# Mean and scale of a LayerNorm spread through DRAM instead of by TensorE's transposes

## The chip, the cores and the metric

The kernel runs on one core of one Trainium2 chip. The metric is device microseconds of one execution; the time of a kernel is the median of its runs. Before the change it is 1457.64 us, the median of three runs (1456.2 to 1458.19).

The core's engines work side by side, each on its own instructions in order: PE (TensorE, matrix products into PSUM), DVE (VectorE, elementwise), ACT (ScalarE, functions and copies), POOL (GpSimd, elementwise, SBUF only) and SP (SyncE, which here issues nearly all DMAs). An instruction that needs another engine's result waits at the head of its engine's queue, and everything behind it waits too.

## The reference

One sequence of 2048 rows of 576 features, all float32:

```python
xn = layernorm(x)                       # over the 576 features, eps 1e-5
q, k, v = split(xn @ wqkv)              # 32 heads of 18 features
pq, pk = phi(q), phi(k)                 # t + 1 where t > 0, else exp(t); + 1e-6
kv = einsum("bhsd,bhse->bhde", pk, v);  z = sum over s of pk
o = (pq @ kv) / (pq . z + 1e-6)         # linear attention, not causal
s = o @ wo
g = silu((gelu(xn @ w_gate) * (xn @ w_up)) @ w_down)
out = x + s * g
```

## The kernel before

The 2048 rows are 16 tiles of 128 rows; four tiles are a block (`TB` = 4 blocks of `TBN` = 512 rows). Products that must be exact to float32 are made from two words: an operand is cut into a high word in a fast matmul type (made by ACT) and a rest (made by DVE with a subtraction), and seven products of words make one of float32 (`PASSES`, `KV_PASSES`). Some short products are plain float32 instead.

**Stage 1** (lines 1328 to 1520) normalises the tiles and makes keys, values and the sum `kv`. For tiles 8 to 15, which the change touches, it does the following per tile t, in `kv_tile` (line 492):

- `x_mm(t, 0)`, `x_mm(t, 1)`, `x_mm(t, 2)`: 14 matmuls each on PE, xn of the tile times a third of the key and value weights, each into a PSUM bank of its own.
- `k_post(t, 0)` and `k_post(t, 1)`: DVE reads the keys out of the banks twice (once for the exponential, `e_k`, once for the positive part, `pk`); after the second, ACT makes the exponential of the whole tile and POOL adds it to `pk`.
- `v_post(t, 1)` and `v_post(t, 2)`: ACT copies the values from the banks to `va`, and some query columns to `qt`; POOL sets a column of ones in `va`.
- `turn(t + 1)`: see below; `place(t + 1)`, which for these tiles is `normalize` (line 228): DVE subtracts the mean from the tile (128 x 768), multiplies each half by the scale (128 x 384, twice), ACT casts the high words of the halves (`hi`), and DVE makes the four rests. `x_mm(t + 1, 0)` needs this.
- In an even tile, after `x_mm(t, 0)`, `kv_pair(t)`: for the two tiles before, `kv_mm` multiplies `pk` by `va` into the accumulator `kv_a`: five groups of heads, each in two halves, the fifth group with a short operand (36 columns, not 72). These are plain float32 products. They need POOL's `pk` and ACT's `va` of both tiles.

From tile 4 on, x comes twice: as rows (for the statistics) and transposed by the host (for the products), in one buffer for two tiles. `load_x(n, 2)` fetches tiles n and n + 1; two buffers alternate, so tiles 12 and 13 are fetched behind tile 8, into the buffer of tiles 8 and 9. Statistics run over the rows: `spread(n0, 2)` has DVE take mean and variance of two tiles (`bn_stats`, `bn_aggr`) and ACT a first inverse root; `scales(n0)` improves it with three small DVE instructions. Then mean and scale of a tile are columns, one number per partition; but in the transposed x a row of the tile runs along the free axis, so the two columns must become rows, equal in all partitions. `turn` does that: two 128 x 128 transposes on PE of a column broadcast to a square, into one PSUM bank `ms`, which `normalize` reads.

Statistics of tiles 12 and 13 are taken by `x_next(12)` at the end of tile 10, those of 14 and 15 by `x_next(14)` at the end of tile 12 (line 1509).

Between tiles 7 and 8 lie the query products of blocks 0 and 1 (`q_store`, line 540: PE makes them, DVE, ACT and POOL apply phi into a `gl` buffer, SP stores it to DRAM). Work of other engines is hung behind single products by the table `behind` (line 1492): there are the statistics of tiles 8 and 9 and of 10 and 11, the turn and place of tile 8, and the forms `T1` to `T4`, sums of x that are cut into words and stored. `form("T4")` runs at the end of tile 9 (line 1511): an ACT cast of 128 x 1536 and two DVE rests. Behind tile 15 follow the query products of blocks 2 and 3 with the table `ahead` (line 1521), the attention output, and then the long gate, up and down products, which take the rest of the span.

The order on every engine is the order of the program text: each helper (`act`, `vec`, `mm`, `pool`, `dma`, lines 122 to 135) pins its instruction in program order. Buffers come from pools by tag: `bank` has six PSUM banks, `gl` six SBUF buffers of 2 KB per partition, `slot` four (in this stage `pk` and `va` of two tiles). A first write to a reused buffer waits for the last reader of its former tile.

Of the kernel before, what the change touches and what calls it, by code (L numbers as in the profile page):

```python
# [8 lines left out]
F32 = mybir.dt.float32  # L9
# [7 lines left out]
P = 128  # L17
# [9 lines left out]
TT = TBN // P  # L27
# [64 lines left out]
def block_kernel(ctx, tc, x, xe, xt, wq_d, wkv_d, wo, wgu_d, wd_d, out):  # L92
# [76 lines left out]
    def spread(n0, n):  # L169

        bn = sb.tile([P, TT, 12], F32, tag="bn", bufs=2, name=f"bn_{n0}")
        mv = sb.tile([P, 2 * TT, 2], F32, tag="mv", bufs=4, name=f"mv_{n0}")
        for t in range(n):
            xs = xstat[(n0 + t) // 2][:, (n0 + t) % 2]
            for j in range(2):
                src = xs[:, j, 0:HALF] if n0 < TT else xs[:, j * HALF : (j + 1) * HALF]
                vec("bn_stats", out=bn[:, t, 6 * j : 6 * j + 6], in_=src)
            vec("bn_aggr", out=mv[:, t, :], in_=bn[:, t, :])
        st = sb.tile([P, 6, TT], F32, tag="st", bufs=4, name=f"st_{n0}")
        act(st[:, 0, 0:n], mv[:, 0:n, 1], AF.Ln, bias=eps_t)  # L180
        act(st[:, 2, 0:n], st[:, 0, 0:n], AF.Exp, scale=-0.5)
        vec("tensor_scalar", st[:, 1, 0:n], mv[:, 0:n, 1], LN_EPS, None, op0=ALU.add)
        mom[n0] = n, mv, st

    def scales(n0):

        n, mv, st = mom.pop(n0)
        v, r, c = (st[:, i, 0:n] for i in range(1, 4))
        if n == 1:
            vec("tensor_scalar", c, r, r, -0.5, op0=ALU.mult, op1=ALU.mult)  # L190
            vec("tensor_scalar", c, c, v, 1.5, op0=ALU.mult, op1=ALU.add)
            vec("tensor_scalar", c, c, r, None, op0=ALU.mult)
        else:
            vec("scalar_tensor_tensor", c, r, -0.5, r, op0=ALU.mult, op1=ALU.mult)
            vec("tensor_mul", c, c, v)
            vec("scalar_tensor_tensor", c, c, 1.5, r, op0=ALU.add, op1=ALU.mult)
        for t in range(n):
            scale_of[n0 + t] = mv[:, t, 0:1], c[:, t : t + 1]

    def center(n):  # L200

# [6 lines left out]
    def turn(n, new=bank):  # L208

        xs = xstat[n // 2][:, n % 2]  # L210
        if n >= TT:
            xts[n] = t = bank(f"ms_{n}")
            for i, v in enumerate(scale_of.pop(n)):
                pin(nc.tensor.transpose(  # L214
                    t[:, i * P : (i + 1) * P], v.to_broadcast([P, P]), ident
                ))
            return
        tiles = [new(f"xt_{n}_{j}") for j in range(2)]
        xts[n] = [t[:, 0 : 3 * P].rearrange("p (k t) -> p k t", k=3) for t in tiles]
        for j in range(2):  # L220
            for k in range(3):
                pin(nc.tensor.transpose(xts[n][j][:, k, :], xs[:, j, k * P : (k + 1) * P], ident))
# [4 lines left out]

    def normalize(n, s, b, c):

        ms = xts.pop(n)  # L230
        xs = xstat[n // 2][:, n % 2, D:].rearrange("p (k t) -> p k t", k=6)
        m, r = (ms[:, None, i * P : (i + 1) * P] for i in range(2))
        vec("tensor_sub", xs, xs, m.to_broadcast([P, 6, P]))
        for j, nm in enumerate(BS[b]):
            if nm not in xo[s]:
                xo[s][nm] = big(2 * b + j, [P, 5, TBN], F32R, f"xo_{s}_{nm}")
                new_plain(s, nm)
            vec(
                "tensor_mul", xf[s][nm][:, :, c], xs[:, 3 * j : 3 * j + 3],
                r.to_broadcast([P, 3, P]),  # L240
            )
        for nm in BS[b]:
            to_operand(xo[s][nm], xf[s][nm], c)
# [32 lines left out]
        if last:  # L276
            xts.pop(n)

    mom, scale_of, xts = {}, {}, {}

    def to_operand(o, src, c):
        act(o[:, 0:3, c], src[:, :, c], AF.Copy)
# [110 lines left out]
        act(e, e, AF.Exp, scale=-1.0)  # L393
        pool("tensor_add", o, o, e)

    def kv_mm(t):
        if t == 0:
            acc.append(own_bank("kv_a"))
        pk, va = pks.pop(t), vas.pop(t)
        for gi, wdt in enumerate(WIDTHS):  # L400
            for half in range(2):
                o, cs = kv_out(gi, half)
                mm(
                    o, va[:, 2 * gi + half, 0 : o.shape[0]],
                    pk[:, gi * GW + cs.start : gi * GW + cs.stop],
                    start=(t == 0 and gi == 0), stop=(t == S // P - 1),
                    skip_group_check=True,
                )
# [8 lines left out]
    def x_mm(t, c, js=(0, 1), passes=KV_PASSES):  # L417

        tb, i = divmod(t, TT)
        s, b = divmod(tb, 2)  # L420
        begin = (t, c) not in pkv
        if begin:
            pkv[t, c] = bank(f"kv_{t}_{c}")
        o = pkv[t, c]
        for j in js:
            for n, (wi, xi) in enumerate(passes):
                mm(
                    o[:, 0 : TW[c]], xo[s][BS[b][j]][:, xi, i * P : (i + 1) * P], kv_part(c, j, wi),
                    start=(begin and j == 0 and n == 0), stop=(j == 1 and (wi, xi) == (2, 2)),
                )  # L430
# [61 lines left out]
    def kv_tile(t, mid_=(), end=()):  # L492

        ahead = t % (2 * TT) != 2 * TT - 1
        x_mm(t, 0)
        if t % 2 == 0:
            kv_pair(t)
        if ahead:
            turn(t + 1)
        k_post(t, 0)  # L500
        x_mm(t, 1)
        if ahead:
            place(t + 1)
            save(t + 1)
        run(list(mid_))
        k_post(t, 1)
        v_post(t, 1)
        x_mm(t, 2)
        run(list(end))
        v_post(t, 2)  # L510

    def kv_pair(t):

        for i in (t - 2, t - 1):
            if i in vas:
                kv_mm(i)

    ph, ph_d = {}, {}

# [958 lines left out]
    def form_apart(nm):  # L1478
# [11 lines left out]
        dma(out=d[:, 2], in_=last[:, 0].bitcast(F32))  # L1490

    behind = {
        (0, 0): [lambda: kv_pair(N0), lambda: spread(N0, 2), lambda: difference(0, 3)],
        (0, 1): [
            lambda: scales(N0), lambda: form("T1"), lambda: q_store(1, 4),
        ],
        (0, 2): [lambda: form_apart("T3")],
        (0, 3): [lambda: turn(N0)],
        (1, 0): [lambda: place(N0)],
# [5 lines left out]
            run(behind.get((tb, gi), []))  # L1505
    for n in range(N0, 2 * N0):
        ends = []
        if n < 2 * N0 - 2:
            ends.append(lambda n=n: center(n + 2) if n == N0 else x_next(n + 2))
        if n == N0 + 1:  # L1510
            ends.append(lambda: form("T4"))
        if n == 2 * N0 - 3:
            ends.append(load_wo)
        if n == 2 * N0 - 2:
            ends.append(make_sel)
        if n == 2 * N0 - 1:
            ends += [lambda i=i: difference(1, i) for i in range(3)]
        kv_tile(n, end=ends)
        if n in (N0, N0 + 2):
            load_x(n + 4, 2)  # L1520
    ahead = {
        (2, 0): [lambda: kv_pair(2 * N0), kv_done, spread_sel, lambda: difference(1, 3)],
        (2, 1): [lambda: kv_wo(4), lambda: q_hold(2, 7, 4)],
        (2, 2): [lambda: kv_wo(0), lambda: kv_wo(1), move_rows],
        (2, 3): [lambda: kv_wo(2), lambda: kv_wo(3)],
        (3, 0): [lambda: den(2), lambda: q_hold(3, 8, 4)],
# [117 lines left out]
```

## Time and profile before

| | |
|---|---|
| median of three runs | 1457.64 us |
| profiled execution, its own time | 1456.24 us |
| span of the profiled execution | 1454.5 us |
| PE busy | 1447.7 us, 100% of the span |
| DVE, ACT, POOL busy | 79%, 39%, 40% |
| DMA moved | 233.98 MB, 161 GB/s over the span |
| granted TensorE clock | 1.00 |

The profile is one execution. Its page gives the busy time of each engine and the groups of instructions that cost most; the trace behind it can be asked for a timeline. A row of a timeline has the start (us from the span's start), the time, the engine, the line of the program, the operation, `out<-in` by the program's names, the shapes, and how many instructions are merged in the row; in brackets stands how long the engine sat idle before it and what ended that. A line is that of the helper (L126 is `vec`, L123 `act`, L132 `pool`, L129 `mm`, L214 the transposes of `turn`), so rows are told apart by their names. Plain float32 products leave two records each: a pair of 20 products shows as x40. A matmul's time runs until its result has left the array, so rows overlap; the distance between starts is what a matmul costs. In the page, "chain that ended last" follows back what released each step.

In time: the query products of blocks 0 and 1 end at 106.6 us, tile 8 begins there, tile 15 ends at 175.2 us.

### The profile page before, as it was taken

How to read it: one execution, taken by the hardware profiler on the slowest of the kernel's cores; microseconds unless marked ns; L12 is line 12 of the kernel's file. 1: busy time of each engine (PE TensorE's matmuls, PEld its weight loads, DVE VectorE, ACT ScalarE, POOL GpSimd, SP SyncE). 2: the span in 40 equal slices, each digit the busy share in tenths (PEclk: the TensorE clock that was granted, in tenths of full speed). 3: DMA queues.
4: the chain of work that ended last, by engine and by line, in shares of the span. 5: the costliest groups of instructions: out<-in, count | busy, mean ns of one | idle time of the engine just before them, and what ended most of it. 6: DMA issues, size and time to landing. Idle time of an engine off the chain costs nothing.

```text
span 1454.5 us, 22180 instructions
## 1 busy us (share of the span) xinstructions
PE 1447.7 (100%) x8286; PEld 1289.9 (89%) x8286; DVE 1149.5 (79%) x1605; ACT 561.3 (39%) x914; POOL 579.6 (40%) x520
## 2 busy tenths in 40 slices
PE   9999999999999999999999999999999999999998
PEld 8989989988888888888888888888889999999998
DVE  7787767376787887888777878778888978989888
ACT  6343355332222233322332232332235555545454
POOL 3342340235756567566475755667632000000000
PEclk9999999999999999999999999999999999999999
DMA  5543105521422315224242243323389887767886
GB/s 223 191 190 141 38 30 212 209 109 51 169 98 104 130 51 182 94 94 140 72 159 87 98 149 106 113 85 118 129 277 349 262 263 251 249 188 232 278 289 224
DMA packets 118085, 233.98 MB, mean 161 GB/s; under 512 B 11018, under 2 KB 44682, under 8 KB 116058
## 3 DMA queue, kind: packets, MB, share of 16 engines
q1 hardware_dynamic: 115178, 220.31, 45.0%
q0 software_dynamic: 2656, 12.06, 2.2%
q8 instruction: 65, 1.06, 0.3%
q14 instruction: 42, 0.34, 0.1%
q10 hardware_dynamic: 144, 0.20, 0.0%
HBM read 149.91 MB, written 82.58 MB: 160 GB/s over the span
## 4 chain that ended last, share of the span: by engine, by line
PE 98%; DVE 1%; ACT 0%; issue 0%; POOL 0%; DVEq 0%; ACTq 0%; POOLq 0%
PE bd L129 25%; PE al L859 16%; PE de L859 16%; PE ga L859 16%; PE kv L129 8%; PE be L859 8%; PE s L129 4%; PE q L129 4%; PE kv_a L129 1%; PE idle L129 0%; PE d L129 0%; PE kw L129 0%; PE b L129 0%; PE ms L214 0%; DVE acc L126 0%
## 5 line engine op out<-in xcount | busy, mean ns | idle before, releaser
L132 POOL TENSOR_TENSOR sm<-raw 128x384 f32<-128x384 f32 x72 | 75.2, 1044 | 145.9 <-DMA raw<-in_wgu_dram 120.6
L129 PE MATMUL kv<-wkv,xo_B 128*128 128x412 f32 (+2 forms) x662 | 125.7, 348 | 0.0
L129 PEld LDWEIGHTS kv<-wkv,xo_B 128*128 128x128 f32 x662 | 119.8, 188 | 1.4 <-DVE wkv L126 0.5
L126 DVE TENSOR_TENSOR wa<-sm,wa 128x768 fp32r<-128x768 f32 x72 | 92.3, 1282 | 36.1 <-ACT wa L123 35.2
L129 PE MATMUL bd<-w_head,hi 128*128 128x288 f32 x516 | 117.9, 294 | 0.0
L126 DVE TENSOR_TENSOR wb<-raw,wb 128x256 fp32r<-128x256 f32 (+1 forms) x108 | 102.1, 946 | 7.4 <-ACT wb L123 5.8
L126 DVE TENSOR_TENSOR wa<-raw,wa 128x256 fp32r<-128x256 f32 x72 | 66.3, 921 | 51.7 <-ACT wa L123 50.6
L123 ACT ACTIVATE hi<-raw_h 128x1024 fp32r<-128x1024 f32 x59 | 62.5, 1060 | 94.8 <-PE bd L129 64.8
L129 PE MATMUL bd<-w_end,hi 128*128 128x288 f32 x448 | 89.8, 294 | 0.0
L123 ACT ACTIVATE spot_h<-spot_h 128x512 f32<-128x512 f32 x49 | 30.7, 633 | 150.3 <-DVE spot_h L126 150.3
L129 PEld LDWEIGHTS bd<-w_head,hi 128*128 128x128 f32 x516 | 87.0, 188 | 0.1
L126 DVE TENSOR_TENSOR raw_h<-raw_h,hi 128x1024 fp32r<-128x1024 f32 x59 | 71.7, 1220 | 17.3 <-ACT hi L123 17.2
L129 PE MATMUL bd<-w_end,raw_h 128*128 128x288 f32 x264 | 77.9, 295 | 0.0
L123 ACT ACTIVATE wa<-sm 128x1152 fp32r<-128x1152 f32 x36 | 41.8, 1161 | 91.8 <-PE de L859 91.8
L123 ACT ACTIVATE u<-al 128x512 f32<-128x512 f32 x72 | 40.9, 593 | 89.5 <-PE al L859 56.3
L129 PEld LDWEIGHTS bd<-w_end,hi 128*128 128x128 f32 x448 | 71.9, 188 | 0.0
L129 PE MATMUL bd<-beside,raw_h 128*128 128x288 f32 x240 | 70.8, 295 | 0.0
L132 POOL TENSOR_TENSOR spot_h<-spot_h,spot_h 128x512 f32<-128x512 f32 x45 | 62.7, 1399 | 2.9 <-DVE spot_h L126 2.4
L859 PE MATMUL al<-xo_B,wa 128*128 128x512 f32 x252 | 63.0, 389 | 0.0
L859 PE MATMUL al<-xr_B,wa 128*128 128x512 f32 x252 | 63.0, 389 | 0.0
L859 PE MATMUL be<-xo_T,wa 128*128 128x512 f32 x252 | 63.0, 389 | 0.0
L859 PE MATMUL be<-xr_T,wa 128*128 128x512 f32 x252 | 63.0, 389 | 0.0
(274 smaller groups left out, 4039.9 us busy)
## 6 DMA issues: line engine op xcount, KB each, us to landing
raw_h<-hs SPq DMA_DIRECT2D x176, 256.0 KB
raw<-in_wgu_dram SPq DMA_DIRECT2D x36, 768.0 KB
hs<-spot_h SPq DMA_DIRECT2D x90, 256.0 KB
hs<-spot_g SPq DMA_DIRECT2D x80, 256.0 KB
b<-in_wd_dram SPq DMA_DIRECT2D x42, 432.0 KB
hs<-spot_m SPq DMA_DIRECT2D x38, 256.0 KB
raw_g<-hs SPq DMA_DIRECT2D x22, 256.0 KB
raw_a<-hs SPq DMA_DIRECT2D x20, 256.0 KB
```

The costliest lines, as they stand in the source:

```text
L123: pin(nc.scalar.activation(*args, **kw))
L126: pin(getattr(nc.vector, op)(*args, **kw))
L129: pin(nc.tensor.matmul(*args, **kw))
L132: pin(getattr(nc.gpsimd, op)(*args, **kw))
L859: nc.tensor.matmul(o, w[0:rows, wi, :], xop[0:rows, xi, :], start=(start and n == 0), stop=(n == len(PASSES) - 1), skip_group_check=True,)
```

## The change

- `scales` has new work for pairs of tiles from 8 on. One DVE copy puts the two means beside the two scales, so that a partition holds four numbers. Two DMAs on SP follow: one writes them to a DRAM tile of 4 rows of 128 numbers (`md`), turning columns into rows, 512 pieces of 4 bytes; the other reads the 2 KB back into all 128 partitions (`mr`, a `gl` buffer, 256 KB in all). For each tile from 9 on, `rows_of` holds the two rows, mean and scale.
- `turn` returns at once for a tile in `rows_of`, so tiles 9 to 15 have no transposes; tile 8 still has. `normalize` takes mean and scale from `rows_of` where there is no `ms` bank.
- In `kv_tile`, `place(t + 1)` of such a tile stands ahead of `k_post(t, 0)`, no longer behind it.
- `x_next(12)` moves from the end of tile 10 into tile 9, between `k_post(9, 0)` and `k_post(9, 1)`; `x_next(14)` from the end of tile 12 to the end of tile 11 (ahead of `v_post(11, 2)`).
- `kv_pair` runs groups 0 to 3 of both tiles first and the short fifth group of both after that; the tiles are released behind both.
- The last query group of block 1, `q_store(1, 4)` (four transposes on PE and one phi), moves to directly behind `kv_pair(8)`; that of block 2, `q_hold(2, 7, 4)`, to directly behind `kv_pair(16)` and `kv_done`.

```diff
@@ scales
+        if n0 >= 2 * TT:
+            vec("tensor_copy", st[:, 3, 2:4], mv[:, 0:2, 0])
+            d = dr.tile([4, P], F32, name=f"md_{n0}")
+            g = gl_tile([P, 4, P], f"mr_{n0}")
+            dma(out=d.rearrange("c t -> t c"), in_=st[:, 3, :])
+            dma(
+                out=g.rearrange("p c t -> p (c t)"),
+                in_=d.rearrange("c t -> (c t)")[None, :].to_broadcast([P, 4 * P]),
+            )
+            for t in range(n):
+                if n0 + t > 2 * TT:
+                    rows_of[n0 + t] = [g[:, None, i + t] for i in (2, 0)]
@@ turn
+        if n in rows_of:
+            return
@@ normalize
-        ms = xts.pop(n)
+        if n in xts:
+            ms = xts.pop(n)
+            m, r = (ms[:, None, i * P : (i + 1) * P] for i in range(2))
+        else:
+            m, r = rows_of.pop(n)
...
-        m, r = (ms[:, None, i * P : (i + 1) * P] for i in range(2))
@@ kv_mm
-    def kv_mm(t):
+    def kv_mm(t, groups):
...
-        for gi, wdt in enumerate(WIDTHS):
+        for gi in groups:
@@ kv_tile
+        early = t + 1 in rows_of
         x_mm(t, 0)
         if t % 2 == 0:
             kv_pair(t)
-        if ahead:
+        if early:
+            place(t + 1)
+        elif ahead:
             turn(t + 1)
         k_post(t, 0)
         x_mm(t, 1)
-        if ahead:
+        if ahead and not early:
             place(t + 1)
             save(t + 1)
         run(list(mid_))
@@ kv_pair
-        for i in (t - 2, t - 1):
-            if i in vas:
-                kv_mm(i)
+        pair = [i for i in (t - 2, t - 1) if i in vas]
+        for groups in (range(4), (4,)):
+            for i in pair:
+                kv_mm(i, groups)
+        for i in pair:
+            del pks[i], vas[i]
@@ behind
-        (0, 0): [lambda: kv_pair(N0), lambda: spread(N0, 2), lambda: difference(0, 3)],
-        (0, 1): [
-            lambda: scales(N0), lambda: form("T1"), lambda: q_store(1, 4),
+        (0, 0): [
+            lambda: kv_pair(N0), lambda: q_store(1, 4), lambda: spread(N0, 2),
+            lambda: difference(0, 3),
         ],
+        (0, 1): [lambda: scales(N0), lambda: form("T1")],
@@ tiles 8 to 15
-        if n < 2 * N0 - 2:
-            ends.append(lambda n=n: center(n + 2) if n == N0 else x_next(n + 2))
+        middle = [lambda: x_next(N0 + 4)] if n == N0 + 1 else []
+        if n == N0 + 3:
+            ends.append(lambda: x_next(N0 + 6))
...
-        kv_tile(n, end=ends)
+        kv_tile(n, middle, ends)
@@ ahead
-        (2, 0): [lambda: kv_pair(2 * N0), kv_done, spread_sel, lambda: difference(1, 3)],
-        (2, 1): [lambda: kv_wo(4), lambda: q_hold(2, 7, 4)],
+        (2, 0): [
+            lambda: kv_pair(2 * N0), kv_done, lambda: q_hold(2, 7, 4), spread_sel,
+            lambda: difference(1, 3),
+        ],
+        (2, 1): [lambda: kv_wo(4)],
```

More of the change, by code (lines that the diff above doesn't have):

```diff
@@ L277, in save @@
             xts.pop(n)
-    mom, scale_of, xts = {}, {}, {}
+    mom, scale_of, xts, rows_of = {}, {}, {}, {}
     def to_operand(o, src, c):
@@ L394, in phi @@
         pool("tensor_add", o, o, e)
-    def kv_mm(t):
-        if t == 0:
+    def kv_mm(t, groups):
+        if not acc:
             acc.append(own_bank("kv_a"))
-        pk, va = pks.pop(t), vas.pop(t)
-        for gi, wdt in enumerate(WIDTHS):
+        pk, va = pks[t], vas[t]
+        for gi in groups:
             for half in range(2):
```

## The prediction

> **What bounds the kernel now.** First the page: how much of the span PE works, and what the last chain is made of.
>
> ```profile
> span 1454.5 us, 22180 instructions
> PE 1447.7 (100%) x8286; PEld 1289.9 (89%) x8286; DVE 1149.5 (79%) x1605; ACT 561.3 (39%) x914; POOL 579.6 (40%) x520
> ```
>
> PE stands still for 6.8 us of 1454.5 us, so a microsecond taken from PE's queue, or put into it, should arrive at the end. Second, who made PE wait:
>
> ```profile
> PE ms L214 <- DVE st L126: 0.8, 1, 0.8
> ```
>
> Outside the start this is the one wait: the turn of tile 12, which needs the statistics that DVE has just made. Third, PE's timeline through tiles 8 to 15:
>
> ```profile
> 106.62 2.80 PE L129 MATMUL kv<-wkv,xo_B 128*128 128x416 f32 x14
> 109.25 0.27 PE L214 MATMUL ms<-ident,mv 128*128 128x128 f32 x1
> ...
> 109.39 7.94 PE L129 MATMUL kv<-wkv,xo_B 128*128 128x412 f32 x42
> 117.17 0.27 PE L214 MATMUL ms<-ident,mv 128*128 128x128 f32 x1
> ...
> 125.23 1.38 PE L129 MATMUL kv_a<-pk,va 128*64 128x72 f32 x40
> 126.54 0.32 PE L214 MATMUL ms<-ident,mv 128*128 128x128 f32 x1
> ...
> 126.73 7.95 PE L129 MATMUL kv<-wkv,xo_B 128*128 128x412 f32 x42
> 134.52 0.27 PE L214 MATMUL ms<-ident,mv 128*128 128x128 f32 x1
> ...
> 135.62 7.95 PE L129 MATMUL kv<-wkv,xo_B 128*128 128x412 f32 x42
> ...
> 162.35 13.01 PE L129 MATMUL kv<-wkv,xo_B 128*128 128x412 f32 x70
> 175.20 1.32 PE L129 MATMUL q<-xo_B,wq 128*128 128x512 f32 x5
> ```
>
> The reader is to see a turn (ms) between runs of kv matmuls, and kv_a, the pair of tiles 8 and 9, at 125.23.
>
> Fourth, DVE in the same stretch:
>
> ```profile
> 110.58 0.69 DVE L126 TENSOR_SCALAR ph<-q 128x512 f32<-128x512 f32 x1 [0.46 <-ACT e_q L123]
> 111.19 0.58 DVE L126 TENSOR_SCALAR e_k<-kv 128x416 f32<-128x416 f32 x1
> ...
> 112.18 0.94 DVE L126 TENSOR_TENSOR x<-x,ms 128x768 f32<-128x768 f32 x1
> 113.16 1.02 DVE L126 TENSOR_TENSOR xf_B<-x,ms 128x384 f32<-128x384 f32 x2
> ...
> 115.84 0.32 DVE L126 TENSOR_SCALAR e_k<-kv 128x160 f32<-128x160 f32 x1
> ...
> 117.44 0.59 DVE L126 TENSOR_SCALAR e_k<-kv 128x416 f32<-128x416 f32 x1 [1.04 <-PE kv L129]
> ...
> 122.23 0.33 DVE L126 TENSOR_SCALAR e_k<-kv 128x160 f32<-128x160 f32 x1
> ...
> 131.77 0.33 DVE L126 TENSOR_SCALAR e_k<-kv 128x160 f32<-128x160 f32 x1
> ...
> 132.35 0.82 DVE L126 BATCH_NORM_STATS2 bn<-x 128x6 f32<-128x288 f32 x2
> ...
> 135.33 0.16 DVE L126 SCALAR_TENSOR_TENSOR st<-st 128x2 f32<-128x2 f32 x1
> 135.41 0.58 DVE L126 TENSOR_SCALAR e_k<-kv 128x416 f32<-128x416 f32 x1
> ```
>
> DVE enters this stage late: it reads the last q bank at 110.58, though PE began tile 8 at 106.62. From there to k_post(9, 1), the e_k at 122.23, it pauses once, for 1.04 us. Prices: place 112.18 to 115.84 = 3.66; k_post(t, 0) 111.19 to 112.18 = 0.99; k_post(t, 1) 131.77 to 132.35 = 0.58; x_next 132.35 to 135.41 = 3.06.
>
> Fifth, what follows k_post(9, 1):
>
> ```profile
> 113.74 0.99 ACT L123 ACTIVATE xo_B<-xf_B 128x384 fp32r<-128x384 f32 x2 [2.53 <-DVE xf_B L126]
> ...
> 122.65 0.69 ACT L123 ACTIVATE e_k<-e_k 128x576 f32<-128x576 f32 x1 [1.52 <-DVE e_k L126]
> ...
> 123.50 1.48 ACT L123 ACTIVATE xo_T<-xf_B 128x1536 fp32r<-128x1536 f32 x1
> 124.88 0.49 ACT L123 ACTIVATE va<-kv 128x252 f32<-128x252 f32 x2
> ```
> ```profile
> 123.42 1.45 POOL L132 TENSOR_TENSOR pk<-pk,e_k 128x576 f32<-128x576 f32 x1 [4.91 <-ACT e_k L123]
> ```
>
> Tile 9's products need POOL's pk (done 124.87, 2.64 after e_k) and ACT's va, which stands behind form T4's cast (done 125.37, 3.14 after e_k; all but its short part some 0.15 sooner, so 3.0). They run in the second half of kv_a, from about 125.23 + 1.31/2 = 125.9. The cover there is half a microsecond.
>
> **The change, part by part.**
>
> *Turns 9 to 15 leave PE.* In an odd tile the run 109.39 to 117.17 (7.78) is c1 + c2 + c0. The run 162.35 to 175.20 (12.85) holds that and c1 + c2 again, 5.07; with c0 = 2.63 (106.62 to 109.25) a tile without a turn takes 7.70. With one, 7.78 + 0.14 (109.25 to 109.39) = 7.92: 0.22 saved. In an even tile, behind kv_a, the next matmul is slow in any case: 126.54 to 126.73, 0.19. Turn 12 with its stall: 134.52 to 135.62 = 1.10, and 0.09 of slow first matmul: 1.19. Sum: 0.22 x 3 (9, 10, 14) + 0.19 x 3 (11, 13, 15) + 1.19 = 2.42.
>
> *Short products last, q_store(1, 4) and q_hold(2, 7, 4) beside kv_pair.* The same instructions in another order. kv_a spends 1.31 on 40 records, 0.033 each; regrouping should save about one record in each of eight pairs, 0.2 (bounds 0, and 0.5 for two). The transposes of those two join plain fp32 work that is there already: 0.05 each (bounds 0 and 0.09, the slow first matmul above). Together 0.3; the ends on PE's side are then -2.7 and 0.
>
> *place(t + 1) moves ahead of k_post(t, 0)* and waits for no PE. The same DVE and ACT work; what is behind it, k_post(t, 0), frees its bank about 3.7 later, and six banks hold two tiles' three. I cost it at nothing: the slack of those banks hides it.
>
> *x_next(12) moves from behind tile 10 into tile 9, in front of k_post(9, 1).* On DVE 3.06, and the new copy 0.16 (the st row at 135.33), 3.2 in all, stand between PE's x_mm(9, 1) and everything that kv_pair(10) needs of tile 9. This is the step that I think decides.
>
> *Mean and scale now lie in SBUF, not PSUM.* The subtraction and both multiplications of place read two SBUF tensors, while POOL adds ph or pk. What that does:
>
> ```profile
> 77.26 6.46 DVE L126 TENSOR_TENSOR xf_B<-xf_B,xf_B 128x1536 f32<-128x1536 f32 x3
> ...
> 86.33 1.75 DVE L126 TENSOR_TENSOR xf_B<-xf_B,xf_B 128x1536 f32<-128x1536 f32 x1
> ```
> ```profile
> 77.85 2.46 POOL L132 TENSOR_TENSOR pk<-pk,e_k 128x576 f32<-128x576 f32 x1 [0.95 <-ACT e_k L123]
> ...
> 110.25 2.55 POOL L132 TENSOR_TENSOR ph<-ph,e_q 128x512 f32<-128x512 f32 x2 [5.71 <-DVE ph L126]
> 117.02 1.43 POOL L132 TENSOR_TENSOR pk<-pk,e_k 128x576 f32<-128x576 f32 x1 [4.22 <-ACT e_k L123]
> ```
>
> Three differences take 6.46, not 3 x 1.75 = 5.25, and POOL's add 2.46, not 1.43: they took turns, and DVE lost 1.2. At 112.18, with ms in PSUM, 0.94 beside POOL's adds (110.25 to 112.80) was undisturbed. So place(9) and place(10), each meeting one add, lose about 1.2 and 1.1 (bounds 0 and 1.43).
>
> The Trainium skill, SBUF — State Buffer, § Who interferes with whom, says that a VectorE instruction with two SBUF inputs contends with a GpSimd one that reads SBUF, and that the second to issue blocks fully; with at most one SBUF input it doesn't. By it the change is slower on DVE, as the rows say; without it the sum is -0.5 (rival 1).
>
> *The DRAM turn.* Eight more issues on SP (four 2 KB writes in 4-byte pieces, four reads of 256 KB), the read held until its write has landed. Behind it on SP stand the last ph stores and the load of x 12 and 13; six gl buffers, two now kept. Nearest rows for issue to landing:
>
> ```profile
> hs<-spot_h POOLq DMA_DIRECT2D x12, 256.0 KB, 4.1
> ```
> ```profile
> 0.80 0.39 SPq L135 DMA_DIRECT2D x<-in_xe_dram  x1
> ...
> 3.51 0.82 DVE L126 BATCH_NORM_STATS2 bn<-x 128x6 f32<-128x288 f32 x2 [3.51 <-DMA x<-in_xe_dram]
> ```
>
> Two of 2.7 (SP) to 4.1 are 5.4 to 8.2; I take 6, since both are on SP. Tile 10's leaves at 109.33 + 0.3 = 109.7 and is wanted when DVE reaches place(10), at 111.4 + 3.66 + 1.2 + 0.99 + 0.58 = 117.8: 8.1. Hidden, narrowly; tile 9's has 20 us.
>
> **The sum on DVE.** After ph at 110.58 (slot 0.61) and the copy 0.16, place(9) starts at 111.4. It meets POOL's second add: its first operand comes at 111.4 + 0.98 (to the multiplications, 112.18 to 113.16) + 1.2 + 0.5 + 0.5 (halves of 1.02 and of the cast's 0.99) = 114.6; PE wants it at 106.62 + 2.63 + 5.07 - 0.1 = 114.2, a stall of 0.4. Work to k_post(9, 1) was 122.23 - 111.19 - 1.04 = 10.0. Now 111.4 + 10.0 + 3.2 + 1.2 + 1.1 = 126.9 to 127.1. Tile 9's parts follow 3.0 later, at 130.1. PE reaches kv_a at 125.23 - 0.44 (turns 9 and 10) - 0.1 + 0.4 = 125.1, does tile 8's half by 125.7 and waits until 130.1: 4.4. Then half a kv_a: x_mm(10, 1) starts at 130.8, not 126.73: +4.1.
>
> From there PE gains turns 12, 13, 14, 15 (1.19 + 0.19 + 0.22 + 0.19 = 1.79) and about 0.15 of order. The next pair, kv_pair(12), finds tile 11 ready within 0.2 of its turn by the same sums. Net 4.1 - 1.95 = +2.1. The profiled execution took 1456.24 beside its span of 1454.5, and 1.4 less than the median 1457.64; against the median the forecast is 1459.7. Measurement tells 0.2% (2.9 us) from nothing; this is 0.15%.
>
> **The rivals.**
> 1. *The shared access doesn't bite*, because POOL's adds fall beside DVE's single-input work. Place(9) and (10) take 3.66, e_k(9, 1) comes at 124.6, tile 9's half at 127.6, x_mm(10, 1) at 128.3: +1.5 - 1.95 = -0.5, 1457.2. For it: POOL works 40%. Against: its add follows each k_post(t, 1), exactly when the next place starts.
> 2. *The change does all that PE's side offers*, -2.7: 1454.9. DVE would have to reach k_post(9, 1) by about 122.7; nothing in the rows frees 4 us there.
> 3. *Slower: the DRAM turn takes over 8.1 us.* place(10) is in order on DVE in front of k_post(9, 0), so each microsecond beyond costs one. By similar sums tile 14's limit is 8.6. At 10: 1.9 + 1.4 more, +5.4, 1463.0. From 8.9 on it is slower by 0.2%. For it: 512 pieces of 4 bytes, of which no row shows the like; against: only 2 KB.
> 4. *Slower: PE's clock falls during the 4.4 us pause.* If it stays halved as long again, 2.2 are lost: 1461.9. No row shows a fallen clock:
>
> ```profile
> PEclk9999999999999999999999999999999999999999
> ```
>
> The Trainium skill, TensorE: Matmul & The Clock Gate, § What's actually happening, has a free-running window of about 3.4 us, after one idle one of which the clock is half: by that, as an estimate, 1.7 lost, 1461.4, if a window falls wholly into the pause.
>
> **Chances.** Forecast 0.56 (own range 1458.2 to 1461.2, a quarter of it above the 1460.6 that is 0.2%), rivals 0.17, 0.05, 0.14, 0.08. Faster by over 0.2% (below 1454.7): half of rival 2, 0.03. Slower: 0.14 + 0.14 + 0.08 = 0.36. Within: 0.61. Range: from near rival 2 to rival 3, 1455.3 to 1463.0.
>
> **What would show it.** Right: DVE's bn for tile 12 near 124 and e_k after it near 127; kv_a's second half behind a PE wait of 3 to 5 us on POOL pk or ACT va; x<-x,mr of tile 10 split from its multiplications by a POOL add; no wait at tile 12. Wrong: kv_a unbroken near 125 (rival 2); DVE waiting on a DMA of mr (rival 3); a granted clock under 1 after 130 (rival 4).

## The result

The changed kernel takes 1476.99 us (median of four runs, 1476.72 to 1477.26) beside 1457.24 us for the kernel before, measured with it: 1.0137 times as long, 95% interval 1.0124 to 1.0149, or 19.7 us more. The forecast was 1459.7 us, the range 1455.3 to 1463.0.

The page of the changed kernel, its span, the engines' busy times, and the granted TensorE clock in 40 slices:

```profile
span 1475.3 us, 22166 instructions
PE 1452.7 (98%) x8272; PEld 1294.0 (88%) x8272; DVE 1156.2 (78%) x1609; ACT 561.7 (38%) x914; POOL 580.6 (39%) x520
PEclk9998999999999999999999999999999999999999
```

PE is busy 5.0 us longer although it has 14 matmuls fewer, and one slice of the clock is below 9. The waits of PE in the changed kernel (who waited, for whom, us in total, times, longest), without the start:

```profile
PE kv L129 <- ACT xo_B L123: 9.5, 3, 6.2
PE kv_a L129 <- POOL va L132: 6.7, 2, 4.9
PE kv_a L129 <- ACT va L123: 0.3, 1, 0.3
```

Where before stood one wait of 0.8, there are six, 16.5 us. 16.5 - 0.8 + 5.0 = 20.7, and the spans differ by 1475.3 - 1454.5 = 20.8: all of the loss stands in these lines. PE's timeline shows where:

```profile
106.74 7.90 PE L129 MATMUL kv<-wkv,xo_B 128*128 128x416 f32 x42
120.86 9.34 PE L129 MATMUL kv<-wkv,xo_B 128*128 128x416 f32 x42 [6.22 <-ACT xo_B L123]
131.62 2.91 PE L129 MATMUL kv<-wkv,xo_B 128*128 128x416 f32 x14 [1.42 <-ACT xo_B L123]
...
140.04 1.47 PE L129 MATMUL kv_a<-pk,va 128*64 128x72 f32 x24 [4.87 <-POOL va L132]
...
175.38 2.91 PE L129 MATMUL kv<-wkv,xo_B 128*128 128x416 f32 x14 [1.90 <-ACT xo_B L123]
...
180.80 0.86 PE L129 MATMUL kv_a<-pk,va 128*64 128x72 f32 x24 [1.86 <-POOL va L132]
181.59 14.64 PE L129 MATMUL kv<-wkv,xo_B 128*128 128x412 f32 x70
```

It waits in front of tile 9 (6.22), tile 10 (1.42), the products of tiles 8 and 9 (4.87), tile 14 (1.90) and the products of 12 and 13 (1.86). A tile's 42 matmuls take 7.90 us in the first row and 9.34 in the second, and the last 70 take 14.64, where the kernel before took 13.01 for them. Windows around two of the waits (window, its length, busy time and instructions of PE, PEld, DVE, ACT, POOL, then the granted clock, DMA share and GB/s) say why:

```profile
120.80:124.20 3.40, 3.34 (x10) 3.20 (x11) 2.96 (x8) 0.89 (x3) 0.00 (x0) 0.55 0.03 5
136.00:142.00 6.00, 1.96 (x26) 1.88 (x27) 3.25 (x10) 3.38 (x8) 1.45 (x2) 0.63 0.04 0
```

The granted clock is 0.55 behind the wait of 6.22, and 0.63 on average over the wait of 4.87 and the products behind it. It falls a third time behind the two waits of 1.9: from 181.6 to 185.0 us it is 0.54.

What the waits hang on is in the chain of work that ended last (start, length, what):

```profile
92.04 10.26 DMA md<-st
102.78 6.42 DMA kept_T<-xo_T
115.93 10.02 DMA md<-st
126.02 3.42 DMA mr<-md
137.48 10.72 DMA md<-st
148.22 3.45 DMA mr<-md
160.28 8.15 DMA md<-st
168.45 4.68 DMA mr<-md
```

Each write of 2 KB takes 8.2 to 10.7 us from issue to landing, each of the three reads back 3.4 to 4.7. The turn is 12.8 to 14.2 us, not 6. It acts in two ways. The first write holds SP, whose next instruction is the read that waits for it; T1's store, behind that read, leaves at 102.78, where before it left at 92.03. T2's cast goes into T1's buffer, so ACT waits, and so does DVE (ACT's row, then DVE's):

```profile
109.22 1.49 ACT L123 ACTIVATE xo_T<-xf_B 128x1536 fp32r<-128x1536 f32 x1 [6.67 <-DMA kept_T<-xo_T]
```
```profile
110.74 1.92 DVE L126 TENSOR_TENSOR xo_T<-xf_B,xo_T 128x1024 fp32r<-128x1024 f32 x2 [7.54 <-ACT xo_T L123]
...
117.51 1.20 DVE L126 TENSOR_TENSOR x<-x,mr 128x768 f32<-128x768 f32 x1
...
129.46 0.96 DVE L126 TENSOR_TENSOR x<-x,mr 128x768 f32<-128x768 f32 x1 [5.53 <-DMA mr<-md]
...
137.36 0.32 DVE L126 TENSOR_SCALAR e_k<-kv 128x160 f32<-128x160 f32 x1
```

DVE reaches place(9) at 117.51, where the forecast had 111.4. The second way is direct: place(10) stands on DVE until its rows come, 5.53 us, and k_post(9, 0), x_next(12) and k_post(9, 1) stand behind it; the e_k at 137.36 was forecast for 127.

### The profile page after: what moved, and what is told of

Read it like the earlier page. It is cut to its first block, busy times and chain, and to the rows that moved or that the text cites. A ratio compares the mean times of both kernels' runs of the same rounds, so it can differ in the third digit from the quotient of the medians.

```text
span 1475.3 us, 22166 instructions
## 1 busy us (share of the span) xinstructions
PE 1452.7 (98%) x8272; PEld 1294.0 (88%) x8272; DVE 1156.2 (78%) x1609; ACT 561.7 (38%) x914; POOL 580.6 (39%) x520
## 4 chain that ended last, share of the span: by engine, by line
PE 92%; DMA 4%; DVE 3%; ACT 1%; issue 0%; POOL 0%; SPq 0%; DVEq 0%; POOLq 0%; ACTq 0%
PE bd L129 24%; PE al L882 15%; PE de L882 15%; PE ga L882 15%; PE be L882 8%; PE kv L129 5%; PE s L129 4%; DMA md<-st 3%; PE q L129 2%; DMA mr<-md 1%; PE kv_a L129 1%; DMA kept_T<-xo_T 0%; DVE bn L126 0%; PE idle L129 0%; PE d L129 0%
## 5 line engine op out<-in xcount | busy, mean ns | idle before, releaser
L129 PE MATMUL kv<-wkv,xo_B 128*128 128x412 f32 (+2 forms) x662 | 129.7, 356 | 9.5 <-ACT xo_B L123 9.5
L129 PEld LDWEIGHTS kv<-wkv,xo_B 128*128 128x128 f32 x662 | 123.9, 194 | 11.9 <-ACT xo_B L123 10.7
L126 DVE TENSOR_TENSOR wb<-raw,wb 128x256 fp32r<-128x256 f32 (+1 forms) x108 | 106.0, 982 | 7.4 <-ACT wb L123 5.8
L882 PE MATMUL ga<-xo_T,wa 128*128 128x512 f32 x252 | 63.0, 389 | 0.0
```

Of the source, the lines that this page charges most:

```text
L126: pin(getattr(nc.vector, op)(*args, **kw))
L129: pin(nc.tensor.matmul(*args, **kw))
L882: nc.tensor.matmul(o, w[0:rows, wi, :], xop[0:rows, xi, :], start=(start and n == 0), stop=(n == len(PASSES) - 1), skip_group_check=True,)
```

## The experiments

Two accounts stood at first: that the turn through DRAM is far longer than costed, or that the early statistics of tile 12, the lock (DVE and POOL taking turns at SBUF) and the clock make the loss, with the turn only a part. The first four kernels take one thing each. A theory named by a number or letter below is that of the expectation just above it. Each ratio is to the kernel before measured beside it, 1456.74 to 1457.5 us, so a difference in us between two of these kernels can be off by up to 0.8.

**Larger pieces.** The four numbers of a partition stay together in DRAM, 128 pieces of 16 bytes instead of 512 of 4; DVE then reads mean and scale in steps of four words.

```diff
-            d = dr.tile([4, P], F32, name=f"md_{n0}")
-            g = gl_tile([P, 4, P], f"mr_{n0}")
-            dma(out=d.rearrange("c t -> t c"), in_=st[:, 3, :])
+            d = dr.tile([P, 4], F32, name=f"md_{n0}")
+            g = gl_tile([P, P, 4], f"mr_{n0}")
+            dma(out=d, in_=st[:, 3, :])
...
-                    rows_of[n0 + t] = [g[:, None, i + t] for i in (2, 0)]
+                    rows_of[n0 + t] = [g[:, None, :, i + t] for i in (2, 0)]
```

> As the changed kernel, but the four numbers of a partition stay together in DRAM (128 pieces of 16 bytes, not 512 of 4), and DVE reads mean and scale with a step of four. Theory 1, the 4-byte pieces make the write slow: the write lands 2 to 4 us after its issue, not 8 to 10.7; no DVE wait for mr, no 6 us wait of PE at tile 9, clock 1.00; what is left is the forecast, 1457 to 1461. Rival, the write is slow because it waits behind other traffic and SP is held whatever the pieces: still 8 us and more, 1474 to 1478.

Measured: 1462.35 us, ratio 1.0037 (1.0024 to 1.0051). This is theory 1, though above its 1457 to 1461. 14.6 of the 19.7 us are gone with the 4-byte pieces: SP's waits for the four writes fall from 37.5 us to 6.7. Of what is left, some shows on PE, as a wait of 4.59 in front of tile 9's products with a fallen clock behind it (the next 84 matmuls take 17.55, the 84 after them 15.72), which theory 1 did not expect, and some on DVE in place(10). The traced execution took 1464.6.

```profile
120.22 1.56 DVE L126 TENSOR_TENSOR x<-x,mr 128x768 f32<-128x768 f32 x1
```

The subtraction takes 1.56 us, where 129.46 above took 0.96: reading the rows in steps of 16 bytes costs DVE 0.6 here. The Trainium skill, SBUF — State Buffer, § Door 1: The DMA port swizzle, says that consecutive accesses within one 16-byte line run at full rate and each step to another line pays; this row agrees.

**No turn.** Rows of constants (mean 0, scale 1, written once by POOL) in place of the turn, so this kernel leaves out the normalisation of tiles 9 to 15.

```diff
-            dma(out=d.rearrange("c t -> t c"), in_=st[:, 3, :])
-            dma(
-                out=g.rearrange("p c t -> p (c t)"),
-                in_=d.rearrange("c t -> (c t)")[None, :].to_broadcast([P, 4 * P]),
-            )
+            if n0 == 2 * TT:
+                at["rows"] = g = gl_tile([P, 4, P], f"mr_{n0}")
+                pool("memset", g[:, 0:2], 1.0)
+                pool("memset", g[:, 2:4], 0.0)
+            g = at["rows"]
```

> As the changed kernel, with no turn through DRAM at all: tiles 9 to 15 take a mean of 0 and a scale of 1 from a buffer set once, so the normalisation of these tiles is left out; every DVE and ACT instruction stays. Theory 1 (the write and what it holds up make up the loss, and the forecast's other steps were right): +2.1 against before, 1458.2 to 1461, one PE wait of 3 to 5 us inside kv_a of tiles 8 and 9, POOL's adds splitting the place of tiles 9 and 10. Rival (the loss is of DVE's order, place ahead of k_post and statistics ahead of k_post(9, 1), the DRAM turn is hidden): 1470 or more. Second rival (all of PE's side): 1454.9.

Measured: 1460.63 us, ratio 1.0027 (1.0015 to 1.0038). So the turn is 16.4 us of the loss (1476.99 - 1460.63). The rest of the change makes 3.5 by itself, and its trace is the prediction's own picture:

```profile
118.48 2.14 DVE L126 TENSOR_TENSOR xf_B<-x,mr 128x384 f32<-128x384 f32 x2
...
126.52 0.32 DVE L126 TENSOR_SCALAR e_k<-kv 128x160 f32<-128x160 f32 x1
```
```profile
129.20 1.48 PE L129 MATMUL kv_a<-pk,va 128*64 128x72 f32 x24 [3.52 <-POOL va L132]
130.61 17.56 PE L129 MATMUL kv<-wkv,xo_B 128*128 128x412 f32 x84
```

e_k(9, 1) at 126.5 (forecast 126.9 to 127.1), tile 9's products at 129.2 (130.1), x_mm(10, 1) at 130.6 (130.8).

**No turn, and the statistics of tiles 12 and 14 at their old places.**

```diff
-        middle = [lambda: x_next(N0 + 4)] if n == N0 + 1 else []
-        if n == N0 + 3:
-            ends.append(lambda: x_next(N0 + 6))
+        middle = []
+        if n in (N0 + 2, N0 + 4):
+            ends.append(lambda n=n: x_next(n + 2))
```

> As the one before (normalisation of tiles 9 to 15 left out), but the statistics of tiles 12 and 14 at their old places, behind tiles 10 and 12. If x_next(12) in front of k_post(9, 1) costs what the forecast says, DVE reaches k_post(9, 1) 3.2 us sooner, the wait inside kv_a falls from about 4.4 to 1.2 us, and the time is 1456 to 1457; if statistics there are hidden, no difference from the one before.

Measured: 1456.38 us, ratio 0.9995 (0.9986 to 1.0004): the 3.5 us hang on the early x_next. Without turn and early statistics the change is level with the kernel before.

```profile
126.98 15.72 PE L129 MATMUL kv<-wkv,xo_B 128*128 128x412 f32 x84
```

The same 84 matmuls as at 130.61 above take 15.72 here and 17.56 there: 1.84 us more behind a pause of 3.5.

**The order of the products alone**, put into the kernel before: `kv_pair` by groups, and the two moves of the fifth query group.

```diff
...
-        (0, 0): [lambda: kv_pair(N0), lambda: spread(N0, 2), lambda: difference(0, 3)],
+        (0, 0): [
+            lambda: kv_pair(N0), lambda: q_store(1, 4), lambda: spread(N0, 2),
+            lambda: difference(0, 3),
+        ],
...
```

> The kernel before with the order of products alone changed: short products last, q_store(1, 4) and q_hold(2, 7, 4) beside kv_pair. Forecast's term: -0.3 us (0 to -0.6), each kv_a block 0.03 us shorter, no new wait. Rival: the moved query group makes DVE later at tile 8 and PE waits there: 0 to +1.

Measured: 1457.18 us beside 1457.08, ratio 1.0000 (0.9991 to 1.0008). The 0.3 us of the forecast can be neither seen nor excluded.

**The pause and the clock.** The kernel without the turn, with 16 matmuls whose result nobody reads between the products of tile 8 and those of tile 9.

```diff
+                if i == 9 and 0 in groups:
+                    o = own_bank("fill")
+                    for k in range(16):
+                        mm(
+                            o[:, 0 : TW[0]], xo[1]["B11"][:, 0, 0:P], kv_part(0, 0, 0),
+                            start=(k == 0), stop=(k == 15),
+                        )
                 kv_mm(i, groups)
```

> The kernel without the DRAM turn (constant rows; the real mean and scale of tiles 9 to 15 are left out), with 16 matmuls more, whose result nobody reads, between the products of tile 8 and those of tile 9: they fill 3.0 of the 3.5 us that PE waits there. Theory A (the pause brings PE half clock for two windows, 1.8 us): no half clock in the trace, the wait below 1 us, 1458.8 us instead of 1460.6. Theory B (the clock of this stage has nothing to do with the pause): half clock as before, 1460.6. Theory C (the matmuls delay the products of tile 9): above 1461.

Measured: 1459.2 us, ratio 1.0016 (1.0007 to 1.0025), against 1.0027 (1.0015 to 1.0038) without them. The times lean to theory A but their intervals overlap; the trace decides:

```profile
125.67 3.28 PE L129 MATMUL fill<-wkv,xo_B 128*128 128x416 f32 x16
129.29 0.96 PE L129 MATMUL kv_a<-pk,va 128*64 128x72 f32 x24 [0.34 <-POOL va L132]
130.18 15.72 PE L129 MATMUL kv<-wkv,xo_B 128*128 128x412 f32 x84
```

The window from 120 to 136 us, first without and then with the 16 matmuls (the granted clock is the first number behind POOL's):

```profile
120.00:136.00 16.00, 12.48 (x87) 11.85 (x86) 12.62 (x33) 5.37 (x12) 1.46 (x2) 0.79 0.26 95
```
```profile
120.00:136.00 16.00, 15.66 (x116) 14.85 (x115) 12.62 (x33) 5.37 (x12) 1.48 (x2) 1.00 0.25 91
```

With PE kept busy the products start at the same time (129.29, without 129.20), and the 84 matmuls behind them take 15.72 again. Behind the pause the clock is 0.50 from 129.2 to 132.6 us; with work without use in its place it stays at 1.00. That is one trace of each.

**The lock.** The kernel without the turn, its constant rows in PSUM instead of SBUF (written by DVE); the edit is shown against that kernel.

```diff
-                at["rows"] = g = gl_tile([P, 4, P], f"mr_{n0}")
-                pool("memset", g[:, 0:2], 1.0)
-                pool("memset", g[:, 2:4], 0.0)
+                at["rows"] = g = own_bank("mr")[:, 0 : 4 * P].rearrange("p (c t) -> p c t", c=4)
+                vec("memset", g[:, 0:2], 1.0)
+                vec("memset", g[:, 2:4], 0.0)
```

> The kernel without the DRAM turn, with the constant rows in PSUM instead of SBUF (the real mean and scale of tiles 9 to 15 are left out); the statistics of tile 12 still early. Theory A (DVE's instructions with two SBUF inputs take turns with POOL's adds, 1.2 and 1.1 us at tiles 9 and 10): the subtraction and multiplications of tiles 9 and 10 at 0.94 and 0.5 us each, kv_a's wait 1.2 to 2 us instead of 3.5, too short for half clock: 1456.5 to 1457.5 us instead of 1460.6, which is rival 1 of the prediction. Theory B (no such lock): the wait stays 3.5 and the time 1460.6.

Measured: 1457.88 us, ratio 1.0006 (0.9997 to 1.0015): 2.8 us less than with rows in SBUF, which had 1.0027 (1.0015 to 1.0038). DVE's multiplications of tile 10, then PE:

```profile
117.71 1.02 DVE L126 TENSOR_TENSOR xf_B<-x,mr 128x384 f32<-128x384 f32 x2
```
```profile
127.31 0.99 PE L129 MATMUL kv_a<-pk,va 128*64 128x72 f32 x24 [1.89 <-POOL va L132]
...
175.02 1.32 PE L129 MATMUL q<-xo_B,wq 128*128 128x512 f32 x5
```

1.02 where the SBUF rows made 2.14, with an add of POOL beside them in both traces (117.31 to 118.75 here, 118.09 to 119.75 there): the lock costs 1.1 us there. At tile 9 it costs 1.3 (subtraction and multiplications take 3.23 with rows in SBUF, 1.96 here). The wait falls from 3.52 to 1.89, and no half clock follows it in this trace.

This is rival 1's condition. In tiles 8 to 15 its picture holds: it put e_k(9, 1) at 124.6 and tile 9's products at 127.6, and they come at 124.63 and 127.31. Its time holds less well: it put it 0.5 us below the kernel before, and this is 1.1 above (-0.4 to 2.2). In the trace the attention behind tile 15 still starts 0.3 us sooner than before (210.30 for 210.60). Two waits of PE on DVE in later stages, 0.7 us each, come after that, and the kernel before has none there; why they come is open.

**SP not held.** The changed kernel, its first read back issued only behind the stores of T1 and T3.

```diff
+            if n0 == 2 * TT:
+                at["read"] = read
+            else:
+                read()
...
-        (0, 3): [lambda: turn(N0)],
+        (0, 3): [lambda: turn(N0), lambda: at.pop("read")()],
```

> The changed kernel, with one edit: the DMA that reads mean and scale of tiles 8 and 9 back is issued on SP only behind the writes of T1 and T3, so that SP does not stand held in front of them; the 4-byte pieces stay. Theory A (the held queue: SP waits 10 us for the write of tile 8, T1's store comes 10 us late, ACT's cast of T2 and with it DVE are late): PE's wait of 6.2 us in front of tile 9 goes below 1; the statistics of tile 10 come about 7 us sooner, their rows still arrive some 5 us too late, so PE waits about 2.7 in front of tile 10, 5 in kv_a, 0.3 and 1.9 and 1.9 after, 11.9 in all instead of 16.6, perhaps with less half clock: 1470.5 to 1472.3 us. Theory B (the latency of the turn itself is all that counts, the held queue costs nothing): no change, 1477. Theory C (the lateness at tile 9 only moves: what is saved there comes back as longer waits at tiles 10 and 12): 1475 to 1477 with the wait at tile 9 gone.

Measured: 1475.65 us, ratio 1.0128 (1.0115 to 1.0142). This is nearest to theory C, though the wait at tile 9 is not gone. PE in front of tile 9, DVE's place(10), then ACT's cast of T2:

```profile
117.48 9.54 PE L129 MATMUL kv<-wkv,xo_B 128*128 128x416 f32 x42 [2.74 <-ACT xo_B L123]
```
```profile
126.84 0.96 DVE L126 TENSOR_TENSOR x<-x,mr 128x768 f32<-128x768 f32 x1 [6.29 <-DMA mr<-md]
```
```profile
105.81 1.49 ACT L123 ACTIVATE xo_T<-xf_B 128x1536 fp32r<-128x1536 f32 x1 [3.16 <-DMA kept_T<-xo_T]
```

The wait at tile 9 falls from 6.22 to 2.74, but place(10) then stands 6.29 us on its rows, not 5.53, and PE's waits in tiles 8 to 15 only fall from 16.5 us to 14.9. The held queue makes more than half of the first wait, yet the latency of the later turns claims most of what it gives back. T1's store now leaves in time, and T2's cast still waits 3.16 us for it. In the next kernel, with the same order on SP and pieces of 16 bytes, it waits for nothing and starts at 102.49. So the small pieces seem to have held up the large transfer behind them as well; that is one trace of each.

**All three mended.** Pieces of 16 bytes, the late first read, and x_next(12) at the end of tile 9, ahead of T4's cast (the last is shown).

```diff
...
-        middle = [lambda: x_next(N0 + 4)] if n == N0 + 1 else []
-        if n == N0 + 3:
-            ends.append(lambda: x_next(N0 + 6))
+        middle = []
+        if n in (N0 + 1, N0 + 3):
+            ends.append(lambda n=n: x_next(n + 3))
```

> The changed kernel with three edits: the turn through DRAM in 128 pieces of 16 bytes, the first read back issued behind the writes of T1 and T3, and the statistics of tile 12 at the end of tile 9 (behind its k_post, ahead of the cast of T4). Theory A (the losses are the 4-byte pieces, the held queue and the early statistics, and nothing else): no PE wait over 1 us, no half clock, 1456.4 us as without any turn (1455.5 to 1457.5), at best 0.1% below the kernel before. Theory B (the turn costs something by itself): waits of 1 to 4 us at tiles 10 or 12, 1458 to 1462.

Measured: 1460.76 us, ratio 1.0026 (1.0016 to 1.0037). Theory A falls, and theory B's range holds: waits of 0.9, 1.4 and 1.7 remain, the 84 matmuls behind the last take 16.81 us, and DVE's place takes the steps of 16 bytes. Whether those steps were all, the next kernel asked: ACT lays each tile's mean and scale into neighbouring words.

```diff
+    def lay(n):
+        g = gl_tile([P, 2, P], f"ml_{n}")
+        for i, v in enumerate(rows_of[n]):
+            act(g[:, i], v, AF.Copy)
+        rows_of[n] = [g[:, None, i] for i in range(2)]
...
+        if early:
+            lay(t + 1)
```

> The kernel of the 16-byte pieces with the later statistics and the later first read (the one that took 1460.8), with one edit: ACT copies the mean and scale of each tile out of the rows of 16-byte steps into rows of neighbouring words, two copies of 128 elements a tile, ahead of the tile's place. Theory A (VectorE reads an operand in steps of 16 bytes slower: subtraction 1.56 us instead of 0.96, multiplications 0.81 instead of 0.51 without POOL beside them, 1.2 us a tile, and that is what was left over): these go back to 0.96 and 0.51, PE waits below 1 us altogether, no half clock, 1456.5 us (1455.5 to 1457.5). Theory B (the turn costs by itself, through the held SP queue and late rows): durations as in A, but the time stays at 1459.5 to 1461. Theory C (ACT, held by its new copies, is late with exponents and casts): waits of 1 to 3 us on xo or va, 1458 to 1462.

Measured: 1460.82 us, ratio 1.0021 (1.0012 to 1.003). The multiplications are back at 1.03 for two, so the steps were the reason for their length, and the time did not follow. Theories B and C both allow it; the waits are theory C's, in ACT's queue. DVE's place(10) stands 1.67 us for ACT's copies. Tile 12's statistics stand there ahead of T4's cast and of tile 9's va, and wait for DVE:

```profile
127.40 0.30 ACT L123 ACTIVATE st<-mv,eps_t 128x2 f32<-128x2 f32 x1 [1.30 <-DVE mv L126]
```
```profile
129.63 1.00 PE L129 MATMUL kv_a<-pk,va 128*64 128x72 f32 x16 [1.73 <-ACT va L123]
130.55 18.05 PE L129 MATMUL kv<-wkv,xo_B 128*128 128x412 f32 x84
```

The clock falls here too, to 0.50 from 129.6 to 133.0 us, and the 84 matmuls take 18.05, more than behind the pause of 3.5. The waits in front of them are of 1.0 and 1.7 us, with 0.5 us of work between. So a fall does not need one long pause, and the length of a single wait does not decide it: one of 1.89 with rows in PSUM brought none.

**The statistics behind the whole of tile 9**, and ACT's copies for tiles 10 and 11 earlier; the edit is shown against the kernel just above.

```diff
-        if early:
+        if early and t + 1 not in (2 * TT + 2, 2 * TT + 3):
             lay(t + 1)
...
+            if t == 2 * TT:
+                lay(t + 2)
+                lay(t + 3)
...
-        if n in (N0 + 1, N0 + 3):
-            ends.append(lambda n=n: x_next(n + 3))
+        if n == N0 + 3:
+            ends.append(lambda: x_next(N0 + 6))
...
+        if n == N0 + 1:
+            x_next(N0 + 4)
```

> The kernel of the 16-byte pieces whose rows ACT lays out, with two edits: the statistics of tile 12 behind the whole of tile 9 (behind T4's cast and both parts of its va on ACT), and ACT's copies for tiles 10 and 11 directly behind the casts of tile 9. Theory A (what was left over came from ACT's order: T4's cast, and behind it tile 9's va, waited for the statistics that stood ahead of them, 1.7 us, and tile 10's copies stood behind tile 8's va, 1.7 us): no PE wait over 1 us, no half clock, 1456.4 us as without any turn (1455.7 to 1457.6), so a turn through DRAM in 16-byte pieces costs PE nothing, and nothing is won by it against the kernel before. Theory B (a turn through DRAM costs 2 to 4 us wherever the rest stands): 1458.5 to 1461, with a wait at tile 10 or 12 that begins with the rows.

Measured: 1460.93 us, ratio 1.0028 (1.0018 to 1.0037). Theory B comes nearer. The wait of 1.73 for tile 9's va is gone, and two others stand in its place on PE, 1.03 us in front of tile 11 and 1.37 in front of that tile's products; behind the second stands a wait of DVE:

```profile
146.90 0.47 PE L129 MATMUL kv_a<-pk,va 128*64 128x72 f32 x8 [1.37 <-POOL va L132]
```
```profile
139.47 0.96 DVE L126 TENSOR_TENSOR x<-x,ml 128x768 f32<-128x768 f32 x1 [2.17 <-ACT ml L123]
```

place(11) is late behind x_next(12). place(12) stands 2.17 us for its rows, whose write left at 132.20, 7.3 us sooner, and tile 11's k_post stands behind it on DVE. So no early place of the statistics came out free: 3.5 us are lost with them in the middle of tile 9 and no turn, and 4.0, 3.3 and 4.1 with them at its end or behind it and a turn in 16-byte pieces. How much of the last three is due to the statistics, to the turn and to rows in SBUF is not separated. In this trace the turn still asks for some 7 us of lead. The old place was free without a turn; a turn from there was not tried.

**What a small write costs.** Eight writes behind the last output of the kernel before, each followed on SP by a read of one of its words.

```diff
+    for n, (k, shape, cut) in enumerate((
...
+        dma(out=cut(d), in_=src)
...
+        dma(out=eps_all[0:1, 20 + n : 21 + n], in_=first)
```

> The kernel before, with eight small writes to DRAM behind its last output, each followed on SP by a read of one word of it, so that the distance between the two issues is the time from issue to landing: in order 512 pieces of 4 bytes as in the changed kernel, 128 of 16, 128 of 4 to neighbouring words, 128 of 4 to words 64 bytes apart, 512 of 4 all 64 bytes apart, 256 of 8, 512 of 16, and the first once more. Only these distances are of interest, the time is longer by their sum. Theory A (the price is by the piece, some 16 to 20 ns each): 8 to 11 us for every 512, 5 for 256, 2 to 3 for every 128, whatever size and distance. Theory B (pieces that fall into the same 64 bytes of DRAM hold each other up): 512 of 4 spread apart land in 2 to 4 us, and 128 of 4 spread apart sooner than 128 to neighbours. Theory C (in the changed kernel they were slow for the other traffic): all of them 2 to 4 us here.

SP's issues in order; a write is `pw<-eps_t`, and the read behind it leaves once the write has landed:

```profile
1453.24 0.44 SPq L135 DMA_DIRECT2D pw<-eps_t  x1
1462.69 0.25 SPq L135 DMA_DIRECT2D eps_t<-pw  x1
1463.29 0.33 SPq L135 DMA_DIRECT2D pw<-eps_t  x1
1465.42 0.24 SPq L135 DMA_DIRECT2D eps_t<-pw  x1
1465.72 0.33 SPq L135 DMA_DIRECT2D pw<-eps_t  x1
1473.45 0.24 SPq L135 DMA_DIRECT2D eps_t<-pw  x1
...
1476.71 0.37 SPq L135 DMA_DIRECT2D pw<-eps_t  x1
1478.48 0.23 SPq L135 DMA_DIRECT2D eps_t<-pw  x1
1478.77 0.37 SPq L135 DMA_DIRECT2D pw<-eps_t  x1
1482.73 0.23 SPq L135 DMA_DIRECT2D eps_t<-pw  x1
```

| write | issue to landing |
|---|---|
| 512 pieces of 4 bytes, as in the changed kernel | 9.45 us |
| 128 pieces of 16 bytes | 2.13 us |
| 128 pieces of 4 bytes, neighbours | 7.73 us |
| 128 pieces of 4 bytes, 64 bytes apart | 2.68 us |
| 512 pieces of 4 bytes, all 64 bytes apart | 1.77 us |
| 256 pieces of 8 bytes, neighbours | 3.96 us |
| 512 pieces of 16 bytes, neighbours | 2.47 us |
| the first once more | 9.42 us |

Theory B. Neither the count nor the size of the pieces sets the time: 512 pieces of 4 bytes take 1.77 us when they lie apart, 128 of them take 7.73 when they are neighbours. Time goes with how many pieces fall into the same stretch of DRAM: in 64 bytes, 16 pieces make 7.7 to 9.5 us, 8 make 4.0, 4 make 2.1 to 2.5, and one makes 1.8 to 2.7. It is not other traffic either: the kernel's own transfers had all been issued, and the last write took 9.42 with nothing issued beside it. How long the shared stretch is was not measured, only that 64 bytes apart is far enough; nor does any run show how the pieces hold each other up. This is one execution.

## Why the prediction was wrong

- **The step that failed** is the DRAM turn, "Two of 2.7 (SP) to 4.1 are 5.4 to 8.2; I take 6 ... Hidden, narrowly". It measured 13.5 at tile 10 (115.93 to 129.46). Both rows it was bounded by move large pieces; the prediction said that no row showed 512 pieces of 4 bytes, and still used those rows as the ends. The read back was near its bounds (3.4 to 4.7); the write, 8.2 to 10.7 for about 3, was not. Rival 3 had the mechanism, with 1463.0 at a turn of 10 us; by its rule of one for one a turn of 13.5 is 5.4 over tile 10's limit of 8.1 and 4.9 over tile 14's of 8.6, so about 1470.0. The rest of the way to 1477 the rule did not count: the wait at tile 9, and the clock.
- **"Tile 9's has 20 us" and the held queue.** Tile 9's rows did come in time. What came late was T1's store behind the held SP queue, and through T2's buffer all of DVE: 6.22 us of PE's waits. The prediction named what stood behind on SP as the last ph stores and the load of x, not T1's store, and followed none to its reader. With the read moved, at most 1.3 us of 19.7 came back (1476.99 to 1475.65, the ratios' intervals overlapping), so this step changed the place of the loss more than its size.
- **x_next(12) in front of k_post(9, 1)**: right. Without the turn its times held within 0.9 us (126.5, 129.2, 130.6), and with x_next at its old place the loss was gone.
- **The lock**: right, in the multiplications of tile 10, 2.14 for 1.02, with 1.1 costed, and at tile 9, 1.3 with 1.2 costed. The Trainium skill, SBUF — State Buffer, § Who interferes with whom, says that a VectorE instruction with two SBUF inputs contends with a GpSimd one that reads SBUF. Both traces agree: with the rows in PSUM the 1.1 us are gone.
- **Rival 4, the clock**, was no rival but an addition: 1.84 us behind a pause of 3.5, where 2.2 were put behind one of 4.4. With it, the net of +2.1 becomes +3.9; the kernel without the turn measured +3.5. The prediction's estimate by the Trainium skill, TensorE: Matmul & The Clock Gate, § What's actually happening, was 1.7, for a window of about 3.4 us that is idle. These traces differ from that condition: two waits of 1.0 and 1.7 us with work between them brought the fall too.
- **PE's savings, 2.42 and 0.3.** From tile 8 to the end of tile 15 the kernel before takes 175.20 - 106.62 = 68.58, and the one with rows in PSUM 175.02 - 106.52 = 68.50, 1.89 of it in a new wait. So 2.0 were saved, the stall at tile 12 among them, of 2.42 and about 0.15 of order. Right in kind; a bit over.
- **place ahead of k_post at nothing**: right as far as these traces show. With the change, PE's waits in tiles 8 to 15 name ACT's xo_B, ACT's va and POOL's va, and never the release of a bank.

## What to carry to other kernels

A column turned into a row through DRAM is a write of many small neighbours: price it by the pieces that share a stretch of DRAM, not by bytes or count, and where no row of the trace resembles it, let the upper bound stay open. When a DMA waits for another on the same queue, follow every transfer behind it to the buffer that it frees. And a latency that must be hidden needs its producer moved ahead: here 3.2 us of DVE in front of other work cost 4.2 us without any turn (1460.63 for 1456.38), more than the 2.0 that the turns on PE had taken.

## What the runs showed of the hardware that was not expected

- Small neighbouring writes to DRAM are slow: 9.45 us for 512 pieces of 4 bytes, 1.77 for the same pieces 64 bytes apart. The Trainium skill, DMA: Bandwidth & Descriptors, § Specifications, says that below 512 bytes a transfer is a read-modify-write; that does not tell these two apart, both being below it.
- DVE reading one of two inputs in steps of 16 bytes: 1.56 us for 0.96 on 128 x 768.
- Sixteen matmuls whose result nobody reads, in a pause of 3.5 us, leave the next 84 at 15.72 us instead of 17.56. Two waits of 1.0 and 1.7 us, with 0.5 us of work between, made the same 84 take 18.05.
